# Sum of phi(k) over the tokens: one product on exchanged partition halves instead of two products on a high and a low part

## The chip, the cores and the metric

The kernel runs on 1 core of one Trainium2 chip. The metric is the device time of that core in microseconds (us). The times are medians of several executions.

Names in the profile: PE is TensorE, DVE is VectorE, ACT is ScalarE, POOL is GpSimd, SPq is the queue of the sync engine, which issues almost all DMA. "L302" is line 302 of the kernel.

## The reference, cut to what matters

`x` has 2048 tokens of 512 values. The kernel computes a gated mix of linear attention (32 heads of 16) and a SwiGLU feed-forward network (FFN).

```python
phi = lambda t: jnp.where(t > 0, t + 1, jnp.exp(t)) + 1e-6
pq, pk = phi(q), phi(k)
kv  = jnp.einsum("bhsd,bhse->bhde", pk, v)
z   = jnp.einsum("bhsd->bhd", pk)                  # sum over all 2048 tokens
num = jnp.einsum("bhqd,bhde->bhqe", pq, kv)
den = jnp.einsum("bhqd,bhd->bhq", pq, z)[..., None] + 1e-6
o   = num / den
...
b   = (silu(x @ w1) * (x @ w3)) @ w2               # FFN
return g * a + (1 - g) * b                         # a = o @ wo, g = sigmoid(x . gate_w)
```

The change concerns only `z`, which every token's `den` needs.

## The kernel before

Tokens lie on the 128 partitions, so the sum over tokens has two parts. GpSimd adds 16 tiles of phi(k) into `pks` (f32, 128x512); then TensorE sums the 128 partitions with a product by a matrix of ones. This product takes bf16 operands, so `pks` is split into a bf16 high part and a bf16 remainder, and two products are accumulated.

The token blocks have 512 tokens. Before the first block, `z` is computed in the middle of that block's FFN, which has ten steps (`fc`). Each step is four gate products and four up products on TensorE, then `th` (ACT), `gs` and `hT` (both DVE):

```python
pks_hi = consts.tile([P, D], BF16, name="pks_hi")
nc.gpsimd.tensor_copy(pks_hi[:], pks[:])
pks_lo = consts.tile([P, D], BF16, name="pks_lo")
nc.gpsimd.tensor_sub(pks_lo[:], pks[:], pks_hi[:])
for fc in range(FC):
    emit_ffn(0, fc)
    if fc == 0:
        z_ps = psX.tile([P, D], FP32, tag="XP1", name="z_ps")
        nc.tensor.matmul(z_ps[:], lhsT=ones_b[:], rhs=pks_hi[:], start=True, stop=False)
        nc.tensor.matmul(z_ps[:], lhsT=ones_b[:], rhs=pks_lo[:], start=False, stop=True)
        nc.scalar.activation(out=z_sb[:], in_=z_ps[:], func=ACT.Copy)
    if 1 <= fc <= TPB:            # TPB = 4 token tiles per block
        emit_den(0, fc - 1)       # qz = pq * z_sb (POOL), den = sum of 16 (DVE)
    if fc == TPB + 1:
        emit_norm(0)              # rden = el / den (DVE x3), pqn = pq * rden (POOL),
                                  # transpose by DMA into pqT
    ...                           # W products at fc 1 and 3
```

```python
def emit_ffn(tb, fc):
    ...
    gate_ps = psM.tile([P, TB], FP32, tag="mm", name="gate_ps")   # psM: 4 PSUM banks
    ...                                                           # 4 products
    up_ps = psM.tile([P, TB], FP32, tag="mm", name="up_ps")
    ...                                                           # 4 products
    nc.scalar.activation(out=th[:], in_=gate_ps[:], func=ACT.Tanh, scale=0.5)
    nc.vector.scalar_tensor_tensor(
        out=gs[:], in0=th[:], scalar=1.0, in1=gate_ps[:], op0=ALU.add, op1=ALU.mult)
    nc.vector.tensor_tensor(
        out=st[tb, "hT"][:, fc, :], in0=up_ps[:], in1=gs[:], op=ALU.mult)
```

There are four PSUM banks for gate and up together. So the gate products of step n+2 must wait until `gs` of step n has read its bank, and the up products of step n+2 until `hT` of step n has. TensorE runs in the order of the program text, but the order of the instructions of the other engines is chosen when the program is built. On each engine it is then fixed.

## Time and profile before

The median was 180.97 us in the first three runs (180.84 to 181.03).

The lines of the page of the kernel before: the span, the busy time of each engine with its share of the span, and the shares of the chain that ended last.

```profile
...
span 179.9 us, 2484 instructions
...
PE 176.0 (98%) x892; PEld 84.7 (47%) x892; DVE 118.9 (66%) x205; ACT 66.7 (37%) x126; POOL 61.2 (34%) x69
...
PE 96%; DVE 2%; issue 0%; DVEq 0%
...
```

TensorE is busy 98% of the span and makes up 96% of the chain. Time is then the number of matmuls times their cadence, plus the gaps on TensorE.

The timeline of the kernel before, TensorE. Columns: start, time from the first start to the last end of the group, engine, line, operation, out<-in, shape, number of instructions. The busy times of matmuls overlap, so read start against start.

```profile
...
41.41 0.38 PE L423 MATMUL z_ps<-pks_hi,ones_b 128*128 128x512 bf16 x1
41.63 0.38 PE L424 MATMUL z_ps<-pks_lo,ones_b 128*128 128x512 bf16 x1
...
47.88 1.03 PE L302 MATMUL gate_ps<-xT,w_sb 128*128 128x512 bf16 x4
48.82 1.02 PE L308 MATMUL up_ps<-xT,w_sb 128*128 128x512 bf16 x4
49.68 1.03 PE L302 MATMUL gate_ps<-xT,w_sb 128*128 128x512 bf16 x4
50.55 1.03 PE L308 MATMUL up_ps<-xT,w_sb 128*128 128x512 bf16 x4
51.62 1.02 PE L302 MATMUL gate_ps<-xT,w_sb 128*128 128x512 bf16 x4
...
```

Four products start every 0.863 us, 0.216 us apart. The gate products of 47.88 are followed after 0.94 us instead (48.82), and the up products of 50.55 after 1.07 us (51.62). These are the only two gaps here, 0.08 and 0.21 us: the first ends when `hT` of step 2 ends, the second when `gs` of step 4 ends.

The timeline of DVE and that of POOL, kernel before. In brackets: how long the engine sat idle before the group, and what ended it.

```profile
...
43.91 0.69 DVE L223 TENSOR_REDUCE den<-qz 128x32 f32<-128x512 f32 x1 [1.05 <-POOL qz L220]
44.52 0.68 DVE L315 SCALAR_TENSOR_TENSOR gs<-th,gate_ps 128x512 bf16<-128x512 bf16 x1
45.11 0.68 DVE L223 TENSOR_REDUCE den<-qz 128x32 f32<-128x512 f32 x1
...
50.08 0.94 DVE L277 RECIPROCAL rden<-rden 128x128 f32<-128x128 f32 x1
50.94 0.63 DVE L315 SCALAR_TENSOR_TENSOR gs<-th,gate_ps 128x512 bf16<-128x512 bf16 x1
...
```

```profile
...
35.45 0.61 POOL L416 CAST pks_hi<-pks 128x512 bf16<-128x512 f32 x1
36.14 1.23 POOL L418 TENSOR_TENSOR pks_lo<-pks,pks_hi 128x512 bf16<-128x512 f32 x1
...
42.72 4.54 POOL L220 TENSOR_TENSOR qz<-pq,z_sb 128x512 f32<-128x512 bf16 x4 [1.92 <-ACT z_sb L425]
51.84 3.08 POOL L285 TENSOR_TENSOR pqn<-pq,rden 128x512 bf16<-128x512 bf16 x3 [4.58 <-DVE rden L278]
...
```

`pks_lo` is done at 37.4, and the z products run at 41.41: 4 us of slack. The reciprocal of 0.94 us at 50.08 stands in front of the `gs` that TensorE waits for at 51.62.

### The profile page before, as it was taken

To read this page: it belongs to the slowest core of one execution; us is meant where nothing else is said; L and a number is where in the kernel's file an instruction comes from. 1 tells how busy PE (TensorE), PEld (TensorE's weight loads), DVE (VectorE), ACT (ScalarE), POOL (GpSimd) and SP (SyncE) were. 2 spreads that over 40 slices of the span, in tenths; PEclk is the share of its full clock that TensorE was granted. 3 is DMA by queue.
4 is the path that set the end of the run, shared out by engine and by line. 5 is a ranking of instruction groups with operands and counts; after the bars stand their busy time and mean duration, and the time that the engine had idled before them with its cause. 6 is when DMAs were issued, how large, how long until landed. Compare 5 with 4: busy or idle time off the path is not lost.

```text
span 179.9 us, 2484 instructions
## 1 busy us (share of the span) xinstructions
PE 176.0 (98%) x892; PEld 84.7 (47%) x892; DVE 118.9 (66%) x205; ACT 66.7 (37%) x126; POOL 61.2 (34%) x69
## 2 busy tenths in 40 slices
PE   8999999999999999999999999999999999999993
PEld 3544444474444545444445454444545444444462
DVE  1497868596998937398777374987764669776000
ACT  4443322476623324243323343333443333331221
POOL 5177665645544323254003232620032327100000
PEclk9999999999999999999999999999999999999999
DMA  6999999901005010105000101240001013300011
GB/s 191 256 253 213 287 343 378 293 13 27 9 0 99 19 47 29 44 29 113 3 4 0 44 29 44 58 89 5 0 7 47 26 55 68 63 0 0 29 51 42
DMA packets 28285, 14.88 MB, mean 83 GB/s; under 512 B 19600, under 2 KB 27248, under 8 KB 28272
## 3 DMA queue, kind: packets, MB, share of 16 engines
q1 hardware_dynamic: 27728, 14.20, 29.3%
q10 hardware_dynamic: 544, 0.52, 0.9%
q8 instruction: 7, 0.11, 0.3%
q14 instruction: 6, 0.05, 0.1%
HBM read 8.42 MB, written 2.10 MB: 58 GB/s over the span
## 4 chain that ended last, share of the span: by engine, by line
PE 96%; DVE 2%; issue 0%; DVEq 0%
PE o_ps L345 19%; PE gate_ps L302 18%; PE up_ps L308 18%; PE XP L199 8%; PE o_ps L336 8%; PE q_ps L212 8%; PE k_ps L179 6%; PE r_ps L236 3%; PE k L179 2%; PE warm L158 2%; PE o_ps L340 2%; DVE hT L318 1%; PE xTp L169 1%; DVE gs L315 1%; PE kvT_ps L406 0%; PE W_ps L433 0%
## 5 line engine op out<-in xcount | busy, mean ns | idle before, releaser
L302 PE MATMUL gate_ps<-xT,w_sb 128*128 128x512 bf16 x160 | 41.1, 379 | 0.0
L308 PE MATMUL up_ps<-xT,w_sb 128*128 128x512 bf16 x160 | 41.1, 379 | 0.0
L220 POOL TENSOR_TENSOR qz<-pq,z_sb 128x512 f32<-128x512 bf16 x16 | 18.5, 1165 | 60.6 <-DVE pq L142 58.7
L313 ACT ACTIVATE th<-gate_ps 128x512 bf16<-128x512 f32 x40 | 23.9, 597 | 38.4 <-PE gate_ps L302 38.0
L345 PE MATMUL o_ps<-w_sb,hT 128*128 128x512 bf16 (+2 forms) x180 | 37.5, 355 | 0.0
L315 DVE SCALAR_TENSOR_TENSOR gs<-th,gate_ps 128x512 bf16<-128x512 bf16 x40 | 27.3, 683 | 6.1 <-ACT th L313 5.8
L318 DVE TENSOR_TENSOR hT<-up_ps,gs 128x512 bf16<-128x512 f32 x40 | 27.6, 691 | 3.7
L139 DVE TENSOR_SCALAR phi_m<-phi_e 128x512 bf16<-128x512 bf16 x32 | 14.9, 466 | 19.6 <-ACT phi_e L137 19.6
L345 PEld LDWEIGHTS <-hT 128*128 128x128 bf16 x180 | 16.8, 97 | 17.9
L308 PEld LDWEIGHTS <-w_sb 128*128 128x128 bf16 x160 | 15.7, 98 | 18.9 <-issue 0.2
L302 PEld LDWEIGHTS <-w_sb 128*128 128x128 bf16 x160 | 15.6, 98 | 18.8 <-issue 0.3
L350 ACT ACTIVATE o_out<-o_ps,omg 128x512 bf16<-128x512 f32 (+2 forms) x17 | 11.1, 656 | 30.4 <-PE o_ps L345 30.4
L285 POOL TENSOR_TENSOR pqn<-pq,rden 128x512 bf16<-128x512 bf16 x16 | 16.6, 1055 | 14.0 <-DVE rden L278 11.7
L189 POOL TENSOR_TENSOR pks<-pks,pk_sb 128x512 f32<-128x512 f32 x15 | 17.3, 1153 | 8.9 <-DVE pk_sb L142 8.4
L223 DVE TENSOR_REDUCE den<-qz 128x32 f32<-128x512 f32 x16 | 11.0, 686 | 8.9 <-POOL qz L220 8.9
L336 PE MATMUL o_ps<-W_sb,pqT 128*128 128x512 bf16 (+2 forms) x72 | 16.8, 355 | 0.0
L212 PE MATMUL q_ps<-wq_sb,xT 128*128 128x512 bf16 x64 | 16.3, 379 | 0.0
L199 PE MATMUL XP<-pk_sb,x_sb 128*128 128x512 bf16 x64 | 16.2, 379 | 0.0
L137 ACT ACTIVATE phi_e<-k_ps 128x512 bf16<-128x512 f32 x12 | 7.2, 597 | 15.4 <-PE k_ps L179 15.4
L179 PE MATMUL k_ps<-wk_sb,xT 128*128 128x512 bf16 x48 | 12.3, 379 | 0.0
L137 ACT ACTIVATE phi_e<-q_ps 128x512 bf16<-128x512 f32 x16 | 9.6, 597 | 7.0 <-PE q_ps L212 5.8
L142 DVE SCALAR_TENSOR_TENSOR pq<-q_ps,phi_m 128x512 bf16<-128x512 f32 x16 | 11.1, 691 | 0.5
(59 smaller groups left out, 121.4 us busy)
## 6 DMA issues: line engine op xcount, KB each, us to landing
w_sb<-in_B_w_dram SPq DMA_DIRECT2D x3, 1280.0 KB, 11.4
out_dram<-o_out SPq DMA_DIRECT2D x15, 128.0 KB, 1.7
x_sb<-in_A_x_dram SPq DMA_DIRECT2D x3, 512.0 KB, 4.5
wk_sb<-in_A_wqkv_dram ACTq DMA_DIRECT2D x2, 256.0 KB, 3.4
wq_sb<-in_A_wqkv_dram SPq DMA_DIRECT2D x1, 512.0 KB, 5.4
wv_sb<-in_A_wqkv_dram SPq DMA_DIRECT2D x1, 512.0 KB, 6.2
wo_sb<-in_A_wo_dram SPq DMA_DIRECT2D x1, 512.0 KB, 12.4
x_sb<-in_A_x_dram SPq DMA_DIRECT2D x2, 128.0 KB, 2.7
```

The costliest lines, as they stand in the source:

```text
L179: nc.tensor.matmul(k_ps[:], lhsT=xT[:, kc, t * P : (t + 1) * P], rhs=wk_sb[:, kc, :], start=(kc == 0), stop=(kc == KC - 1),)
L189: nc.gpsimd.tensor_add(pks[:], pks[:], pk_sb[:, t, :])
L199: nc.tensor.matmul(XP_ps[dc][:], lhsT=x_sb[:, t, dc * P : (dc + 1) * P], rhs=pk_sb[:, t, :], start=(t == 0), stop=(t == NT - 1),)
L212: nc.tensor.matmul(q_ps[:], lhsT=xT[:, kc, ts_tok], rhs=wq_sb[:, kc, :], start=(kc == 0), stop=(kc == KC - 1),)
L220: nc.gpsimd.tensor_tensor(out=qz[:], in0=st[tb, "pq"][:, tt, :], in1=z_sb[:], op=ALU.mult)
L302: nc.tensor.matmul(gate_ps[:], lhsT=w1_sb[:, kc, fsl], rhs=xT[:, kc, tok_sl], start=(kc == 0), stop=(kc == KC - 1),)
L308: nc.tensor.matmul(up_ps[:], lhsT=w3_sb[:, kc, fsl], rhs=xT[:, kc, tok_sl], start=(kc == 0), stop=(kc == KC - 1),)
L313: nc.scalar.activation(out=th[:], in_=gate_ps[:], func=ACT.Tanh, scale=0.5)
L315: nc.vector.scalar_tensor_tensor(out=gs[:], in0=th[:], scalar=1.0, in1=gate_ps[:], op0=ALU.add, op1=ALU.mult)
L318: nc.vector.tensor_tensor(out=st[tb, "hT"][:, fc, :], in0=up_ps[:], in1=gs[:], op=ALU.mult)
L336: nc.tensor.matmul(o_ps[:], lhsT=st[tb, "pqT"][:, c, tsl], rhs=W_sb[:, c, a:b], start=(c == 0), stop=False,)
L345: nc.tensor.matmul(o_ps[:], lhsT=st[tb, "hT"][:, fc, tsl], rhs=w2_sb[:, fc, a:b], start=False, stop=(fc == FC - 1),)
```

## The change

If both partition halves hold the sum of the two halves, the upper 64 partitions can carry the bf16 high part and the lower 64 the remainder, and one product over 128 partitions yields `z`. The halves of `pks` are exchanged by two SBUF to SBUF DMA transfers. Because the exchange takes time, the product, the `den` reductions and the normalization move one FFN step later, and the product moves to another PSUM bank.

```diff
-    pks_hi = consts.tile([P, D], BF16, name="pks_hi")
-    nc.gpsimd.tensor_copy(pks_hi[:], pks[:])
-    pks_lo = consts.tile([P, D], BF16, name="pks_lo")
-    nc.gpsimd.tensor_sub(pks_lo[:], pks[:], pks_hi[:])
+    HP = P // 2
+    pks_x = consts.tile([P, D], FP32, name="pks_x")
+    dq.dma_start(out=pks_x[0:HP, :], in_=pks[HP:P, :])
+    dq.dma_start(out=pks_x[HP:P, :], in_=pks[0:HP, :])
+    nc.gpsimd.tensor_add(pks[:], pks[:], pks_x[:])
+    pks_hl = consts.tile([P, D], BF16, name="pks_hl")
+    nc.gpsimd.tensor_copy(pks_hl[:], pks[:])
+    nc.gpsimd.tensor_sub(pks_hl[HP:P, :], pks[HP:P, :], pks_hl[HP:P, :])
     for fc in range(FC):
         emit_ffn(0, fc)
-        if fc == 0:
-            z_ps = psX.tile([P, D], FP32, tag="XP1", name="z_ps")
-            nc.tensor.matmul(z_ps[:], lhsT=ones_b[:], rhs=pks_hi[:], start=True, stop=False)
-            nc.tensor.matmul(z_ps[:], lhsT=ones_b[:], rhs=pks_lo[:], start=False, stop=True)
+        if fc == 1:
+            z_ps = psX.tile([P, D], FP32, tag="XP2", name="z_ps")
+            nc.tensor.matmul(z_ps[:], lhsT=ones_b[:], rhs=pks_hl[:], start=True, stop=True)
             nc.scalar.activation(out=z_sb[:], in_=z_ps[:], func=ACT.Copy)
-        if 1 <= fc <= TPB:
-            emit_den(0, fc - 1)
-        if fc == TPB + 1:
+        if 2 <= fc <= TPB + 1:
+            emit_den(0, fc - 2)
+        if fc == TPB + 2:
             emit_norm(0)
```

## The prediction

> **What bounds the kernel.** TensorE. The page has PE busy 176.0 of 179.9 us (98%), its clock granted in full, and 96% of the chain that ended last is PE. Time is the number of matmuls times their cadence, plus PE gaps. The timeline's start times give four 512-column matmuls per 0.865 us, 0.216 us each. The Trainium skill, "TensorE: Matmul & The Clock Gate", "Step-by-step: what each phase is for", gives 216 ns back to back; the trace agrees.
>
> **What the change touches** (timeline, 34 to 60 us). The last POOL add into pks ends at 35.4, pks_hi takes 0.61 and pks_lo 1.23 (done 37.4). PE does the two z products at 41.41 and 41.63, after the first FFN pair: z has 4 us of slack. ACT copies z_sb at 42.04, POOL starts qz at 42.72, DVE den at 43.91, pqn starts at 51.84, and the output product reads the first transposed pqn at 60.07.
>
> **Removed:** one 512-column matmul, 0.216 us of the PE stream, all on the critical path.
>
> **Added, off PE:** two exchanges of 128 KB, SBUF to SBUF, on the SP queue; one POOL f32 add (1.15 us, as each pks add). Cast and subtraction stay.
>
> **The new path to z.** SP is idle from 31.6 to 40.3, so the exchanges issue at about 35.5 and 36.0 (0.4 to 0.6 us each). The bulk loads still fill the same queue: DMA share is 1.0 up to 35 us, 0.39 in 35 to 36, 0.13 in 36 to 37, 0.04 until 38. 128 KB loads and stores landed in 1.7 to 2.7 us. The skill, "DMA: Bandwidth & Descriptors", "Rules for kernel authors", says transfers to disjoint partition halves serialize; no run shows that yet. I estimate landing at 38 to 38.7, the add to 39.7, cast to 40.3, subtraction to 41.6; the two hr products (0.55 each, ready at 39.75) may get in between: 42.6. The single product now stands after the second FFN pair, at 41.41 + 1.73 = 43.14, so its operand is 0.5 to 1.5 us early. Moving it by one FFN step pays for the exchange.
>
> **What moves.** z_sb, qz, den and norm come about 1.7 us later; pqn starts at about 53.5, its first transpose lands (2.5 us) at about 57.3, before 60.07. DVE is full from 44 to 56.7 us and already costs PE a little (starts at 48.82 and 51.62 are 0.08 and 0.21 late). The shifted den reductions no longer use the pause around the first W products; those gaps may grow by 0 to 0.3 us and eat the gain. z's new bank XP2 is free since about 36.
>
> **Predicted:** 180.9 us (180.97 - 0.22 + about 0.15), eight in ten within 180.5 to 181.8. Faster by over 2%: 1%; within: 93%; slower: 6%.
>
> **What would show it.** Right: PE has one matmul fewer; pks_x lands before 39; pks_hl is finished before 43; the z matmul starts on PE's cadence; PE gaps between FFN groups in 43 to 55 us sum to 0.3 to 0.6 us. Wrong: a PE gap before the z matmul (released by POOL), or the exchanges issued behind the hTr transposes.
>
> **What would make it wrong.** (1) If POOL puts both hr products before the add, or the exchange lands after 39.7, pks_hl is done at about 43.9 and PE waits 0.8 us: 181.6. (2) If SP issues the hTr transposes first (they hold SP from 40.33 to 45.7), z is ready near 51 and PE waits about 8 us: 189. Unlikely: POOL already runs pks_hi before hr, against program order, so instructions are ordered by readiness. (3) The DVE backlog costs up to 0.5 us more.

## The result, and the profile after

| | median us | lowest to highest | runs |
|---|---|---|---|
| before | 181.03 | 180.84 to 181.74 | 6 |
| after | 181.80 | 181.55 to 181.89 | 6 |

The ratio after to before is 1.003 (95% interval 1.0011 to 1.005). A ratio is the mean time of one kernel's fast runs over that of the other's fast runs of the same rounds, so it is not quite the ratio of the medians. The difference is 0.3%: the same within 2%, but a small loss and not a gain.

The same lines of the page, kernel after:

```profile
...
span 179.8 us, 2488 instructions
...
PE 175.8 (98%) x891; PEld 84.5 (47%) x891; DVE 119.6 (67%) x205; ACT 66.5 (37%) x126; POOL 62.5 (35%) x70
...
PE 93%; DVE 3%; POOL 1%; issue 0%; ACT 0%; DVEq 0%
...
```

There is one matmul fewer (891), yet less of the chain is TensorE: 93% after 96%. The span of this one trace is not longer than the one of before, because its start was luckier: the first XP product ran at 9.37 us, against 9.67 us. Spans of single traces are therefore not compared below; stretches inside them are.

The timeline of the kernel after, TensorE:

```profile
...
42.84 0.38 PE L427 MATMUL z_ps<-pks_hl,ones_b 128*128 128x512 bf16 x1
...
46.94 0.59 PE L436 MATMUL W_ps<-wo_sb,kvT_sb 128*128 128x512 bf16 x2
47.59 1.02 PE L302 MATMUL gate_ps<-xT,w_sb 128*128 128x512 bf16 x4
48.78 1.02 PE L308 MATMUL up_ps<-xT,w_sb 128*128 128x512 bf16 x4 [0.17 <-DVE hT L318]
49.64 1.03 PE L302 MATMUL gate_ps<-xT,w_sb 128*128 128x512 bf16 x4
...
52.29 1.03 PE L308 MATMUL up_ps<-xT,w_sb 128*128 128x512 bf16 x4
53.36 1.02 PE L302 MATMUL gate_ps<-xT,w_sb 128*128 128x512 bf16 x4
...
```

The z product runs on the cadence at 42.84. The gaps come later. Two W products take 0.43 us, so the gate products (step 4) were due at 47.37 and ran at 47.59. The up products were due at 48.45 and ran at 48.78, and the line names what ended the wait: `hT` on DVE. The gate products of step 7, due at 53.15, ran at 53.36. (A fourth gap, at 50.57, is 0.07 us.) The gap at 53.36 has the cause that the gap at 51.62 had before: the `gs` at 52.68 stands behind the reciprocal. The other three are new or larger.

The timeline of DVE and that of POOL, kernel after:

```profile
...
45.12 0.69 DVE L223 TENSOR_REDUCE den<-qz 128x32 f32<-128x512 f32 x1 [0.69 <-POOL qz L220]
46.25 0.69 DVE L223 TENSOR_REDUCE den<-qz 128x32 f32<-128x512 f32 x1 [0.44 <-POOL qz L220]
46.85 0.68 DVE L315 SCALAR_TENSOR_TENSOR gs<-th,gate_ps 128x512 bf16<-128x512 bf16 x1
...
48.04 0.68 DVE L318 TENSOR_TENSOR hT<-up_ps,gs 128x512 bf16<-128x512 f32 x1
...
51.82 0.94 DVE L277 RECIPROCAL rden<-rden 128x128 f32<-128x128 f32 x1
52.68 0.63 DVE L315 SCALAR_TENSOR_TENSOR gs<-th,gate_ps 128x512 bf16<-128x512 bf16 x1
...
```

```profile
...
38.16 1.35 POOL L419 TENSOR_TENSOR pks<-pks,pks_x 128x512 f32<-128x512 f32 x1 [3.07 <-DMA pks_x<-pks]
39.58 0.61 POOL L421 CAST pks_hl<-pks 128x512 bf16<-128x512 f32 x1
40.27 1.15 POOL L422 TENSOR_TENSOR pks_hl<-pks,pks_hl 64x512 bf16<-64x512 f32 x1
...
43.93 4.53 POOL L220 TENSOR_TENSOR qz<-pq,z_sb 128x512 f32<-128x512 bf16 x4 [1.38 <-ACT z_sb L428]
53.58 3.09 POOL L285 TENSOR_TENSOR pqn<-pq,rden 128x512 bf16<-128x512 bf16 x3 [5.12 <-DVE rden L278]
...
```

The exchange landed for the add at 38.16, and `pks_hl` was done at 41.42, in time. But `qz` begins 4.55 us after the first gate product (39.38) instead of 3.04 us (42.72 less 39.68). On DVE two `den` reductions now stand in front of the `gs` at 46.85. DVE idles 0.69 and 0.44 us before them. During the second pause (45.81 to 46.25) that `gs` already has its input, since 45.32, when its `th` ended on ACT. This `gs` ends at 47.53 and the `hT` at 48.04 ends at 48.72: 0.06 us later TensorE goes on each time.

### A measure that repeats

The kernel is cut at three places on TensorE: the first gate product of FFN step 0, the first q product of the second token block (the "stretch" between these two holds all of the change's products), and the first gate product of the second block. The fourth mark is the start of the last group of output products. The two marks of the stretch in the timeline of TensorE, kernel after (58.54 less 39.38 is 19.16 us):

```profile
...
39.38 1.03 PE L302 MATMUL gate_ps<-xT,w_sb 128*128 128x512 bf16 x4
...
58.54 1.03 PE L212 MATMUL q_ps<-wq_sb,xT 128*128 128x512 bf16 x4
...
```

Two kernels below (before_pinned and mid_pinned_w2late) have no gap in the stretch that start times show: 86 matmuls in 18.56 us and 85 in 18.35 us, so 0.2158 us each. "Gaps" in the table is the stretch less 18.56 or 18.35 us. All values are us, one trace each. The matmuls are counted in the program: the traces of after_again, delay_only, hi_only and after_pinned lack two of these records each, and a missing record looks like a gap of 0.21 us between groups.

| kernel | matmuls in stretch | stretch | gaps | next segment | first gate to last product |
|---|---|---|---|---|---|
| before | 86 | 18.84 | 0.28 | 17.79 | 136.49 |
| after | 85 | 19.16 | 0.81 | 17.78 | 136.80 |
| after_again | 85 | 19.14 | 0.79 | 17.79 | 136.79 |
| delay_only | 86 | 19.36 | 0.80 | 17.78 | 137.01 |
| hi_only | 85 | 18.62 | 0.27 | 17.79 | 136.27 |
| after_pinned | 85 | 18.57 | 0.22 | 18.37 | 136.79 |
| den_early_pinned | 85 | 18.67 | 0.32 | 17.79 | 136.32 |
| before_pinned | 86 | 18.56 | none | 17.78 | 136.20 |
| before_pinned_again | 86 | 18.56 | none | 17.79 | 136.21 |
| exch_no_delay | 85 | 20.17 | 1.82 | 17.79 | 137.82 |
| exch_no_delay_again | 85 | 19.02 | 0.67 | 17.78 | 136.66 |
| exch_no_delay_w2late | 85 | 18.98 | 0.63 | 17.79 | 136.63 |
| mid_pinned_w2late | 85 | 18.35 | none | 17.78 | 135.99 |

Traces of the same kernel agree within 0.02 us in these columns, unless the exchange lands late (exch_no_delay). The rest after the second block's first gate product took 99.85 to 99.87 us in all of them. What varies from run to run is the very start: the first XP product ran between 8.85 and 10.36 us. This is why medians of whole runs, with spreads of about 1 us, hardly resolve what the segments show to a few hundredths.

So the sum of the change is known: 0.22 us less for the product, 0.53 us more for gaps in the stretch, together 0.31 us more. The timed loss of 0.3% (0.54 us, interval 0.2 to 0.9 us) agrees with it.

### The profile page after: what moved, and what is told of

Its sections match the earlier page's. It is cut to its first block, busy times and chain, and to the rows that moved or that the text cites. A ratio compares the mean times of both kernels' runs of the same rounds, so it can differ in the third digit from the quotient of the medians.

```text
span 179.8 us, 2488 instructions
## 1 busy us (share of the span) xinstructions
PE 175.8 (98%) x891; PEld 84.5 (47%) x891; DVE 119.6 (67%) x205; ACT 66.5 (37%) x126; POOL 62.5 (35%) x70
## 4 chain that ended last, share of the span: by engine, by line
PE 93%; DVE 3%; POOL 1%; issue 0%; ACT 0%; DVEq 0%
PE o_ps L345 19%; PE up_ps L308 17%; PE gate_ps L302 17%; PE XP L199 8%; PE o_ps L336 8%; PE q_ps L212 8%; PE k_ps L179 6%; PE r_ps L236 3%; PE k L179 2%; PE warm L158 2%; PE o_ps L340 2%; POOL qz L220 1%; DVE hT L318 1%; DVE gs L315 1%; PE xTp L169 1%; PE kvT_ps L406 0%
```

## The experiments

The theories at the start:

- **A, the delay.** `z` comes one FFN step later, and DVE pays. In the version A1 the order in DVE's stream is the reason; in A2 DVE has too much to do in that stretch, whatever the order.
- **B, the exchange.** Its transfers, or GpSimd's additional work and the SBUF port that it shares with DVE, slow the stretch. The Trainium skill, "SBUF — State Buffer", "SBUF: two separate sides", says that GpSimd and some kinds of DVE operation lock each other out of a shared pair of ports for a whole instruction. The traces have signs of it: in after, a DVE operation on 128x4 values took 0.72 us at 40.73 (0.15 us before) and ended at 41.45, just after GpSimd's subtraction at 41.42; in after_again, one on 128x2 values took 1.23 us and ended at 40.78, just after GpSimd's addition at 40.74.
- **C** was added later: the exchange stands in its DMA queue behind bulk loads.

The first four kernels ran on one chip with 11 runs of before (median 181.15 us), den_early_pinned, before_pinned and exch_no_delay on a second one (before 181.18 us), the last four on the second one again (before 181.05 us).

### after_again: the changed kernel, unedited

> The changed kernel once more, unedited, as the yardstick of this batch. In the first traces the stretch from the first gate product of FFN step 0 to the first q product of the second token block took 18.84 us before and 19.16 us after, although it holds one matmul less; PE gaps in it (the stretch less its matmuls at 0.216 us each) were 0.25 and 0.78 us. All theories expect this trace to repeat 19.16 within 0.05 us and the time to be 0.1 to 0.5% above before. If the stretch instead varies by 0.3 us from run to run, the loss is noise and not the change.

Measured: correct; 181.46 us median, ratio 1.0017 (0.9995 to 1.0039). The stretch repeated: 19.14 us. The loss is no noise of one trace. In this trace the exchange landed late (the add began at 39.48) and `pks_hl` was done at 42.66 us, where the z product ran at 42.8. The reserve was nearly used up, but no wait arose.

### delay_only: the delay without the exchange

```diff
-        if fc == 0:
-            z_ps = psX.tile([P, D], FP32, tag="XP1", name="z_ps")
+        if fc == 1:
+            z_ps = psX.tile([P, D], FP32, tag="XP2", name="z_ps")
             ...                                # both products, as before
-        if 1 <= fc <= TPB:
-            emit_den(0, fc - 1)
-        if fc == TPB + 1:
+        if 2 <= fc <= TPB + 1:
+            emit_den(0, fc - 2)
+        if fc == TPB + 2:
             emit_norm(0)
```

> The kernel before with only the delay: both z products (high and low) one FFN step later, in bank XP2, den and norm one step later; no exchange, no saved matmul. Theory A (the delay does it: the den reductions now stand in VectorE's stream in front of a gs whose bank PE needs): gaps of about 0.78 us as in after, stretch 19.16 + 0.22 = 19.38 us, time about 0.5 us (0.3%) above before. Theory B (the exchange does it: DMA traffic[...]): gaps stay at about 0.25 us, stretch 18.84 us, time equal to before.

Measured: correct; 181.78 us, ratio 1.0032 (1.0011 to 1.0053). Stretch 19.36 us, gaps 0.80 us. The timelines of DVE and TensorE of this kernel show the same picture as after: idle in front of two reductions, the `gs` behind them, then the late gate and up products.

```profile
...
45.38 0.69 DVE L223 TENSOR_REDUCE den<-qz 128x32 f32<-128x512 f32 x1 [1.05 <-POOL qz L220]
46.50 0.69 DVE L223 TENSOR_REDUCE den<-qz 128x32 f32<-128x512 f32 x1 [0.43 <-POOL qz L220]
47.10 0.68 DVE L315 SCALAR_TENSOR_TENSOR gs<-th,gate_ps 128x512 bf16<-128x512 bf16 x1
...
```

```profile
...
47.83 1.02 PE L302 MATMUL gate_ps<-xT,w_sb 128*128 128x512 bf16 x4
49.02 1.02 PE L308 MATMUL up_ps<-xT,w_sb 128*128 128x512 bf16 x4 [0.17 <-DVE hT L318]
...
```

The whole of the gaps comes with the delay, without any exchange. Theory B falls: the signs of the shared port can be seen in the trace after, but they cost TensorE nothing measurable here (gaps 0.81 us with the exchange, 0.80 us without). This run moved the PSUM bank as well (XP2); mid_pinned_w2late below keeps that bank and has no gap, so the bank is not the cause.

### hi_only: the product alone

```diff
-            nc.tensor.matmul(z_ps[:], lhsT=ones_b[:], rhs=pks_hi[:], start=True, stop=False)
-            nc.tensor.matmul(z_ps[:], lhsT=ones_b[:], rhs=pks_lo[:], start=False, stop=True)
+            nc.tensor.matmul(z_ps[:], lhsT=ones_b[:], rhs=pks_hi[:], start=True, stop=True)
```

> The kernel before with the low product taken out and nothing moved, so z is rounded to bf16 sums (a slightly less exact result on purpose). This measures the removed matmul alone. If one 512-column product is worth its cadence, stretch 18.84 - 0.22 = 18.62 us with gaps still about 0.25 us, and the time 0.1% below before. If the saving only turns into a later wait for VectorE, the stretch stays nearer 18.8 us.

Measured: 180.95 us, ratio 0.999 (0.997 to 1.001). The outputs are right. Stretch 18.62 us, 0.22 us less than before, and gaps as before. The product is worth its cadence to the end of the kernel (136.27 against 136.49 us).

### after_pinned: the order on DVE

`issue_after` adds an order between two instructions of one engine, without a wait.

```diff
-        nc.vector.tensor_tensor(
+        st["last_hT"] = nc.vector.tensor_tensor(
             out=st[tb, "hT"][:, fc, :], in0=up_ps[:], in1=gs[:], op=ALU.mult
         )
 ...
-            emit_den(0, fc - 2)
+            with tc.issue_after(st["last_hT"].ins):
+                emit_den(0, fc - 2)
```

> The changed kernel with one edit: each den reduction of the first block is issued on VectorE behind hT of the same FFN step. Order only; no work or wait is removed. In the trace of after two reductions stand ahead of the gs of FFN step 2 and VectorE idles 0.44 us in front of the second one while that gs is ready. Theory A1 (the order in VectorE's stream): gaps fall from 0.78 to 0.3 us or less, stretch about 18.4 to 18.7 us, time 0.1 to 0.3% below before. Theory A2 (VectorE simply has too much work in that stretch, whatever its order): gaps stay at 0.6 to 0.8 us, stretch about 19.1 us. Theory B (exchange and port): also unchanged, about 19.1 us.

Measured: correct; 181.59 us, ratio 1.0023 (1.0003 to 1.0043). The stretch fell to 18.57 us as A1 says, but the time did not fall: the next segment grew from 17.79 to 18.37 us. The timeline of TensorE of this kernel shows where:

```profile
...
58.67 0.84 PE L236 MATMUL r_ps<-wr_sb,xT 128*128 128x193 bf16 x8
59.93 1.04 PE L336 MATMUL o_ps<-W_sb,pqT 128*128 128x512 bf16 x4 [0.41 <-DMA pqT<-pqn]
...
```

The first output product was due 0.68 us after the r products (59.35) and ran at 59.93. The bracket names the transposed `pqn`. With the reductions later in DVE's stream, normalization began 56.31 us into the trace (first `pqn` on GpSimd) instead of 53.58. The loss had only moved: from a PSUM bank to the next use of `den`. The expectation was half right; the total is 136.79 us, as after.

### den_early_pinned: the reductions one step earlier

Against the change:

```diff
-        if 2 <= fc <= TPB + 1:
-            emit_den(0, fc - 2)
-        if fc == TPB + 2:
+        if 1 <= fc <= TPB:
+            with tc.issue_after(st["last_hT"].ins):
+                emit_den(0, fc - 1)
+        if fc == TPB + 1:
             emit_norm(0)
```

A build without the `issue_after` gave DVE exactly the instruction order of after, so it was not run: the place in the text did not decide.

> The changed kernel with the z product where it is, but each den reduction of the first block issued on VectorE behind hT one FFN step earlier than in after_pinned (den 0 behind hT of step 1, before gs of step 2), and norm one step earlier. after_pinned showed a stretch of 18.57 us but gave 0.58 us back where the first output product waited for the late transposed pqn. Theory A1 (order in VectorE's stream and the lateness of norm are the whole loss): stretch 18.4 to 18.5 us, the next segment up to the second block's first gate product back at 17.79 us, first gate product to last product about 136.05 us (before 136.49, after 136.80), time 0.1 to 0.3% below before. If the exchange itself cost anything, the sum stays at 136.3 us or more.

Measured: correct; 181.10 us, ratio 1.0009 (0.9976 to 1.0041), one run at 182.68. The late output product is gone (17.79 us), and 136.32 us is 0.48 us better than after, but not the 136.05 us expected. One gap of 0.33 us stayed:

```profile
...
52.97 1.03 PE L308 MATMUL up_ps<-xT,w_sb 128*128 128x512 bf16 x4
54.16 1.02 PE L302 MATMUL gate_ps<-xT,w_sb 128*128 128x512 bf16 x4 [0.17 <-DVE gs L315]
...
```

The gate products were due at 53.83. The `gs` that frees their bank ended at 54.11, behind the reciprocal (52.62 to 53.56). So A2 holds in part: with `z` late, DVE waits for `qz` (0.73 us idle before the first reduction at 44.68) and has no pause above 0.11 us from there to 59.07, so it is behind when the reciprocal comes. Part of this is the pinned order itself: an `hT` directly behind its own `gs` starts 0.78 us after it, while instructions that do not depend on each other start 0.60 us apart (46.85, 47.45 and 48.04 in the trace after). Three such pairs stand before the reciprocal, 0.18 us each. Whether another order would have had no gap with `z` as late was not tried, so how much of the 0.33 us is lateness alone stays open.

### before_pinned and before_pinned_again: the order without the change

The same edit of `emit_ffn`, and `with tc.issue_after(...)` around `emit_den(0, fc - 1)` in the kernel before.

> The kernel before with only the pinning: den k of the first block issued on VectorE behind hT of step k + 1; both z products stay. This separates what the order gives from what the change gives. Theory A1: the gaps of 0.25 us shrink to 0.15 us or less, stretch 18.6 to 18.75 us, next segment 17.79 us, first gate product to last product 136.25 to 136.4 us; den_early_pinned is then better by about the one product, 0.22 us. If it is not better, the exchange costs what the product saves.

> before_pinned once more, on the same chip as mid_pinned_w2late: the order alone, without the change. First trace: stretch 18.56 us, first gate product to last product 136.20 us. Expected to repeat within 0.03 us; the time within 0.2% of before. mid_pinned_w2late should be shorter by 0.15 to 0.2 us from first gate product to last product, the one product.

Measured: both correct; 181.40 us, ratio 1.0014 (0.9993 to 1.0035), then 180.81 us, ratio 0.9977 (0.9956 to 0.9999). The two traces are alike: stretch 18.56 us, no gap, 136.20 and 136.21 us. The two ratios differ by 0.4% for one and the same kernel, which shows how much the start of the run blurs small differences. Against the expectation, this beat den_early_pinned by 0.12 us although it has one product more. The order on DVE is the same in both; the first reduction starts 5.25 us after the first gate product here, and 5.74 us in den_early_pinned.

### exch_no_delay and exch_no_delay_again: the exchange without the delay

The change, with product, `den` and normalization at the steps of before (and bank XP1).

> The exchange and single product of the change without the delay: product, den and norm at the FFN steps of before (bank XP1). In the trace of after GpSimd finishes pks_hl 2.04 us after the first gate product starts, and the product would be due 1.73 us after it. So PE waits about 0.35 to 0.45 us in front of the z product, released by GpSimd; VectorE's order is again that of before, whose gaps were 0.25 us. Stretch 18.84 - 0.22 + 0.4 = about 19.0 us (18.95 to 19.25), next segment 17.79 us, time within 0.2% of before. If the wait is under 0.2 us, the delay by one step was not needed; if over 0.6 us, the hr products or the DMA get into the path.

> exch_no_delay once more, unedited: PE waits in front of the z product for exactly as long as the exchange is late, so its times show how much the exchange varies. Its first six times were 180.95 to 183.97 us, in two groups 2 us apart; the exchange landed 2.2 to 2.8 us after its issue in two traces and 3.6 to 4.0 us in three others. Theory C (the exchange stands in the SP queue behind the end of the bulk weight loads, so its landing depends on when these finish): again two groups, or a spread of over 1 us. If it stays within 0.6 us, the first spread was that one call's chance.

Measured: correct; first 182.13 us, ratio 1.0043 (0.9995 to 1.0092), runs from 180.95 to 183.97 (this last one slow; the median of the five fast runs alone is 181.15 us); then 181.68 us, ratio 1.0031 (1.0008 to 1.0054), runs from 181.06 to 182.29. The stretch was 20.17 us in the first trace, a miss, and 19.02 us in the second, as expected. The two groups did not come back; a spread of 1.2 us did, though before spread over 0.9 us. The first trace, timelines of TensorE and POOL:

```profile
...
41.25 1.03 PE L308 MATMUL up_ps<-xT,w_sb 128*128 128x512 bf16 x4
43.68 0.38 PE L427 MATMUL z_ps<-pks_hl,ones_b 128*128 128x512 bf16 x1 [1.40 <-POOL pks_hl L422]
...
```

```profile
...
40.46 1.26 POOL L419 TENSOR_TENSOR pks<-pks,pks_x 128x512 f32<-128x512 f32 x1 [4.36 <-DMA pks_x<-pks]
...
```

The z product was due at 42.11 and waited for `pks_hl` until 43.68, 1.57 us. The cause of this wait is the exchange: it landed 3.6 to 3.9 us after issue. It is not all of the late group: the traced run took 183.54 us, 2.48 us more than the second (181.06 us), and of this 1.15 us lie in the stretch and 1.18 us before the first XP product (10.36 against 9.18 us). In the traces the landing goes with the end of the last bulk load in the queue, the remainder of w2 (its issue plus its time to landing):

| kernel | last bulk load landed | exchange: time to landing | POOL add began |
|---|---|---|---|
| after | 35.7 | 2.2 to 2.3 | 38.16 |
| exch_no_delay_again | 37.3 | 2.4 to 2.6 | 38.0 |
| after_pinned | 37.6 | 2.5 to 2.8 | 38.28 |
| den_early_pinned | 38.1 | 3.6 to 3.8 | 39.01 |
| after_again | 38.7 | 3.7 to 4.0 | 39.48 |
| exch_no_delay | 39.7 | 3.6 to 3.9 | 40.46 |

The Trainium skill, "DMA: Bandwidth & Descriptors", "Queues, rings and completion order", says that each DMA engine takes the descriptors of a ring in order. These numbers agree with it: both transfers are on the SP queue, and where the bulk loads end late, the exchange lands shortly behind them; where they end early, it needs its own 2.2 us. They do not show whether the order in the queue or merely the busy DMA engines held it up: no run put the exchange on another queue.

### exch_no_delay_w2late: the exchange ahead of the last bulk load

```diff
-    dq.dma_start(out=w2_sb[:], in_=B_w2[0:FM, :].rearrange("(fc f) d -> f fc d", f=P))
-    dq.dma_start(out=w2r_sb[:FR, :], in_=B_w2[FM:F, :])
 ...
-    dq.dma_start(out=pks_x[HP:P, :], in_=pks[0:HP, :])
+    x2 = dq.dma_start(out=pks_x[HP:P, :], in_=pks[0:HP, :])
+    with tc.issue_after(x2.ins):
+        dq.dma_start(out=w2_sb[:], in_=B_w2[0:FM, :].rearrange("(fc f) d -> f fc d", f=P))
+        dq.dma_start(out=w2r_sb[:FR, :], in_=B_w2[FM:F, :])
```

> exch_no_delay with one edit: the last two bulk loads of the SP queue (w2, 1280 KB, and its remainder), first needed some 20 us later, are issued behind the exchange instead of ahead of it. Theory C: the exchange finds the queue empty and lands 2.0 to 2.6 us after issue, pks_hl is done about 2.0 us after the first gate product starts, PE waits 0.3 to 0.45 us, stretch about 19.0 us, and the times spread over less than 1 us, none above 182.2 us. If landing still takes 3.6 us or the times still fall in two groups, the queue is not the cause (rival: SBUF to SBUF traffic or GpSimd itself varies).

Measured: correct; 181.05 us, ratio 0.9997 (0.9974 to 1.0019), runs from 180.85 to 181.74. Timelines of TensorE and POOL:

```profile
...
39.85 1.03 PE L306 MATMUL up_ps<-xT,w_sb 128*128 128x512 bf16 x4
41.09 0.38 PE L428 MATMUL z_ps<-pks_hl,ones_b 128*128 128x512 bf16 x1 [0.21 <-POOL pks_hl L423]
...
```

```profile
...
37.80 1.32 POOL L420 TENSOR_TENSOR pks<-pks,pks_x 128x512 f32<-128x512 f32 x1 [3.10 <-DMA pks_x<-pks]
...
```

Both transfers landed in 2.3 us. The product was due at 40.71 and ran at 41.09: a wait of 0.38 us, which is the price of the exchange without the delay. 18.98 us is 18.84 less the product (0.22) plus this wait. Every expectation of theory C was met (moving w2 clears both the queue and the DMA engines). That the late group of exch_no_delay came from the queue in all its runs is not shown, since only one of them was traced.

### mid_pinned_w2late: everything together

Against the change: w2 behind the exchange, `den` pinned as in den_early_pinned, and the z product between gate and up of step 1.

```diff
-    def emit_ffn(tb, fc):
+    def emit_ffn(tb, fc, mid=None):
         ...                                    # the gate products
+        if mid is not None:
+            mid()
         up_ps = psM.tile([P, TB], FP32, tag="mm", name="up_ps")
 ...
-        emit_ffn(0, fc)
-        if fc == 1:
-            ...                                # z product and copy
+        emit_ffn(0, fc, emit_z if fc == 1 else None)
```

> Everything that the runs point to, with the change kept: exchange ahead of w2, the z product between the gate and up products of FFN step 1 (0.86 us earlier than in the change), each den k pinned on VectorE behind hT of step k + 1. If A1 and C are right: no wait in front of z, gaps of 0.1 us or less, stretch 18.35 to 18.5 us, next segment 17.79 us, first gate product to last product 136.0 to 136.1 us (before 136.49, before_pinned 136.20). Time about 0.2% below before. Rival A2 (VectorE's load alone): a gap of 0.2 to 0.3 us remains at the reciprocal and the sum is 136.3 us, as in den_early_pinned.

Measured: correct; 180.50 us (180.06 to 181.20), ratio 0.9966 (0.9942 to 0.999). The timeline of TensorE around the z product:

```profile
...
40.47 1.03 PE L300 MATMUL gate_ps<-xT,w_sb 128*128 128x512 bf16 x4
41.33 0.38 PE L429 MATMUL z_ps<-pks_hl,ones_b 128*128 128x512 bf16 x1
41.55 1.03 PE L308 MATMUL up_ps<-xT,w_sb 128*128 128x512 bf16 x4
...
```

There is no wait before the product, no gap in the stretch (18.35 us), and 135.99 us to the last product: 0.50 us less than before, 0.81 us less than after. Against before_pinned_again it is shorter by 0.22 us, the one product. So, by one trace of each, the change does pay 0.22 us, once the delay that it brought is cut and DVE's order is right; whole times (180.50 against 180.81 us, with spreads of 1.1 and 0.8 us) are too coarse to show this. The first reduction starts 5.15 us after the first gate product here, earlier than in before_pinned. As several things were altered together, this run does not say what each would give alone.

## Why the prediction was right or wrong

The time of 181.8 us lies at the upper edge of the range of 180.5 to 181.8, and the class "within 2%" was right. The central value was 0.9 us too low for this set of runs and, more to the point, had a tiny gain where there was a small loss. About 0.4 us of this is the term named below; the other 0.5 us do not show in the segments, which put after only 0.31 us behind before, and after_again was 0.31 us above before. How near to the edge the time came is thus partly the chance of the start.

- **The product is worth 0.216 us, all on the critical path: right.** hi_only measured 0.22 us.
- **The exchange fits into the delay: right in the first trace, with less reserve than stated.** Predicted were a landing at 38 to 38.7 and the end of `pks_hl` at 41.6; the trace has 38.16 for the add and 41.42. But the landing was read as one number. It depends on when the bulk loads end (2.2 to 4.0 us over the traces), and in after_again the reserve had shrunk to 0.1 us.
- **SP would not issue the exchange behind the transposes: right.** GpSimd ran the two `hr` products after `pks_hl`.
- **`pqn` would begin at about 53.5 and cause no wait: right** (53.58).
- **"those gaps may grow by 0 to 0.3 us": the term that failed.** They grew by 0.53 us (0.28 to 0.81), and after_again and delay_only repeated it. So the prediction's own sign, gaps of 0.3 to 0.6 us in all, was missed by 0.2 us. The mechanism was right, and the size was not: the prediction put 0.15 us into its sum and left "up to 0.5 us more" to its list of risks. The prediction saw that DVE was full and that the delay would cost there, but it did not work out the new order of DVE's instructions. In the built program a second reduction had moved in front of `gs` of step 2, and in that place DVE idled for `qz` while TensorE needed the `gs`. after_pinned and den_early_pinned show the order's part. The gap that stayed in den_early_pinned, and was gone in mid_pinned_w2late, where `z` came 0.86 us earlier in the same DVE order, shows that under this order the lateness matters too: idle DVE time before `qz` is missing later, when the reciprocal comes.

With 0.53 instead of the predicted growth the same sum gives a loss of 0.3 us, which is what the segments show.

## What to carry to other kernels

Moving a product later to hide the latency of its operand is not free only because the busiest engine meets no wait there: follow what hangs on the product (here `qz`, `den`, the normalization) to the engine that serves the PSUM banks, and ask whether it has idle time later to catch up. A fixed instruction order on such an engine decides which of two consumers waits, so pin it, and check the next deadline after that: after_pinned only moved the loss. Look also at what the pinned order costs the engine itself (here 0.18 us for each `hT` directly behind its `gs`). A small transfer whose time matters should not be queued behind bulk loads that are needed more than 20 us later.

## What the Trainium skill lacked or had wrong

- "DMA: Bandwidth & Descriptors", "Anatomy of one DMA": the fit there (2.0 us plus bytes over 436 GB/s, about 2.3 us as an estimate for 128 KB) is given for transfers issued by GpSimd. For SBUF to SBUF transfers on the SP queue the traces have the same 2.3 us when nothing is ahead in the queue. The page gives no figure for what bulk loads ahead in the same queue add; here up to 1.7 us (4.0 us in after_again).
- The same page, "Rules for kernel authors", says that transfers to disjoint partition halves serialize. No run here decides it: the two exchanges were issued 0.6 us apart and both landed 2.3 us after their own issue.
- "TensorE: Matmul & The Clock Gate", "Back-to-back issue gap", gives about 131 ns per 512-column matmul for a stream of weight loads and matmuls, and says that 216 ns over-counts there. In this kernel, which is such a stream, it is 0.2158 us per matmul without gaps (86 in 18.56 us). The 216 ns of the section "Step-by-step: what each phase is for" fit.
- "GPSIMD Engine Reference" has no figure for instructions on fewer partitions. The subtraction on 64 partitions took 1.15 us, against 1.23 us on 128 (before) and 1.15 us for an f32 addition on 128: half the partitions saved almost nothing.
- No page looked up here has a figure for what the order of instructions on VectorE can cost TensorE through PSUM banks. It was worth 0.29 us in the kernel before (136.49 against 136.20 us).
